# Changeover between two feed-forward layers: one weight conversion later, a load asked for earlier, output tiles kept apart

## The chip, the cores and the metric

One core of a Trainium2 chip runs the whole program. The metric is the device time in microseconds (us) of one execution; three runs of the kernel before took 1017.71, 1018.67 and 1021.01 us, and the median is 1018.67 us. All the arithmetic is in fp32, and the matrix products are built from fp32r halves ("hi" and "lo" of a number), three matmuls for one product.

## The reference

Causal attention with a bias from a cumulative sum (4 batches, 8 heads, 576 positions, head dimension 64), then two feed-forward layers on 2304 tokens, 512 wide, 2048 hidden:

```python
x = attention(q, k, v, s)              # -> (2304, 512)
h = x @ w_in1;  g = max(h, 0) + alpha * min(h, 0);   y = g @ w_out1
h = y @ w_in2;  g = h * clip(h + 3, 0, 6) / 6;       out = g @ w_out2
```

The weights arrive as float64 and are turned into fp32 on the chip.

## The kernel before, in words

Attention and layer one are interleaved (lines 744 to 818). Layer one runs over blocks of 256 tokens; its last pass, which the change touches, takes the last two blocks at once, 512 tokens (`moe1`, line 660, called at line 850). For each of 16 slices f of the hidden width it makes 12 matmuls into a bank `h` (line 248), then ScalarE and VectorE turn `h` into `gt` (lines 697 and 698), ScalarE rounds it to `gh` (line 701), VectorE makes the rest `gl` (line 702), and 12 matmuls add `gh` and `gl` into the four banks `y` (line 675). The y products of a slice follow the h products of the next one (skew 1). After slice 15 the four banks are copied to `yt` tiles (line 684, pool `stg`, two buffers) and stored to the scratch tensor `y_scratch` (line 686). `f` below counts these slices: gt14 is `gt` of slice 14.

During this last pass the weights of layer two's first product are loaded and converted, in eight pairs, called p0 to p7 here (`load_pair`, line 192; `split_pair`, line 213, called from `more_w2`, line 723). The raw words `wraw` are float64. A conversion of a pair is, per half: ScalarE line 142 writes `wcv`, GpSimd lines 144 and 147, VectorE line 152, and then the low bits, by VectorE at line 155 or by ScalarE at line 150 (`by`, chosen by the last argument of `to_f32`). GpSimd then forms sums `ws` (lines 180 to 183), and ScalarE and VectorE split everything into hi and lo `wc` (lines 160 and 161). `ws` has one buffer, which the token sums `yt` of layer two share (tag "ws").

Layer two's first product uses a scheme of seven products instead of eight (`Step`, line 856). Tokens go in four groups g of 576, hidden columns in eight places j, one pair of weights each; `order` (line 954) begins with group 0, j = 0 to 2, then group 1, all j. A step is 42 matmuls of 128x288 (line 872) in the banks a, b and c, ended by ScalarE copies to `z` and `m5` (`held`, line 879), VectorE additions (`plus`, line 882), and the gate (lines 885 and 886) into `gt2` tiles that are stored to `g_scratch` (line 891). In the trace m5 appears as m and gt2 as gt. The tokens of a group are read back from `y_scratch` (`load_x`, line 826; DMA line 832 into `yr`, two buffers), summed by GpSimd (lines 187 to 190) and split (lines 160 and 161) into x. Groups 0 and 1 use different x tiles; the one of group 1 lies where tiles of layer one's last pass were.

The last phase (lines 1007 to 1039) multiplies the stored g by the second weights w_out2, 16 slices f per block of 512 tokens. These weights are loaded by `load_out` into tiles of first-layer weights that are free (`places`, line 934) and converted by `split_out`.

Memory is given out by pools as stacks from the left and the right side. `stg` is the first pool of the stack `layer1`, which is closed at line 854; pool `m2` of layer two (z, three buffers, and gt2, four) is opened on the left right after that, and so lies where `stg` was. Instructions are put in order on each engine when the program is built; the order follows the text with priorities (`tc.high_priority`), and a converted pair that stands in layer two's loop (line 971) can be placed earlier than the loop's first matmul. All these DMAs are issued by the SP queue, one after the other; an issue that waits holds those behind it.

## Time and profile before

| what | value |
|---|---|
| median of three runs | 1018.67 us (1017.71 to 1021.01) |
| the profiled execution, its own time | 1021.8 us |
| its span, first to last instruction | 1020.0 us |
| TensorE matmuls busy | 984.2 us (96%), 6218 matmuls |
| VectorE, ScalarE, GpSimd busy | 619.9, 630.0, 443.4 us |
| mean granted clock of TensorE | 0.977 of full speed |
| chain of waits, share of TensorE | 90% |

The busy times are of one profiled execution, which took 3.1 us more than the median of the three runs. TensorE is busy nearly all the time, so the time of the kernel is the sum of TensorE's work and of the stretches in which TensorE waits or runs at its lower clock. The layers change over between 611 and 650 us of the span.

### The profile page before, as it was taken

Reading aid. Unit: us, or ns where it says so; the run is one execution under the profiler, and the core shown is the slowest. Engines: PE = TensorE matmul, PEld = TensorE weight load, DVE = VectorE, ACT = ScalarE, POOL = GpSimd, SP = SyncE. Lnnn points to the kernel's source line nnn. Section 1 sums busy time; section 2 is a strip of 40 time slices with the busy share of each in tenths; the row PEclk is TensorE's granted clock in tenths of the full one; section 3 lists DMA queues with packets and bytes.
Section 4 is the critical chain, followed back from the end, with each engine's and each line's share of the span. In section 5 each row is a group of like instructions: output and inputs, shape, how many; then the busy total and the mean of one; then the engine's idle time right before and its main releaser. Section 6 shows DMA issues by size and latency. Waiting matters only on the chain.

```text
span 1020.0 us, 18068 instructions
## 1 busy us (share of the span) xinstructions
PE 984.2 (96%) x6218; PEld 883.1 (87%) x6218; DVE 619.9 (61%) x1507; ACT 630.0 (62%) x1429; POOL 443.4 (43%) x587
## 2 busy tenths in 40 slices
PE   8889999999999999999999996999999999999998
PEld 5568788999999989998998884999999988888886
DVE  5678884556766666666656895757667872222222
ACT  6568778678778788777755544656657653232322
POOL 5554667657667666657636765402203220000000
PEclk9779999999999999999999998899999999999999
DMA  6890014112212122222106321334337733332412
GB/s 209 290 356 4 24 30 130 40 46 89 75 62 84 53 80 68 64 83 75 33 8 215 96 94 58 142 124 150 118 146 279 273 129 124 115 133 83 161 59 90
DMA packets 59829, 114.47 MB, mean 112 GB/s; under 512 B 5705, under 2 KB 21881, under 8 KB 59737
## 3 DMA queue, kind: packets, MB, share of 16 engines
q1 hardware_dynamic: 59736, 113.32, 33.6%
q8 instruction: 49, 0.80, 0.3%
q14 instruction: 44, 0.35, 0.1%
HBM read 84.84 MB, written 28.46 MB: 111 GB/s over the span
## 4 chain that ended last, share of the span: by engine, by line
PE 90%; DVE 2%; ACT 2%; issue 2%; DMA 1%; POOL 1%; SPq 0%; ACTq 0%; POOLq 0%; DVEq 0%
PE o L1029 19%; PE h L248 19%; PE y L675 19%; PE a L872 10%; PE b L872 5%; PE s L410 4%; PE pv L472 4%; PE pt L447 4%; PE c L872 3%; PE s L322 1%; PE pv L603 1%; DMA wraw<-in_w_in 1%; PE pt L593 1%; PE h L534 1%; DVE wcv L152 1%
## 5 line engine op out<-in xcount | busy, mean ns | idle before, releaser
L248 PE MATMUL h<-xhi,wi 128*128 128x256 f32 (+1 forms) x896 | 227.7, 322 | 2.8 <-DVE gt L698 1.6
L1029 PE MATMUL o<-wo,gh 128*128 128x512 f32 x576 | 173.7, 389 | 1.1 <-DVE gt L886 1.1
L248 PEld LDWEIGHTS h<-xhi,wi 128*128 128x128 f32 x896 | 156.9, 192 | 16.2 <-DVE gt L698 1.9
L675 PE MATMUL y<-gh,wo 128*128 128x256 f32 (+1 forms) x896 | 164.0, 318 | 4.8 <-ACT gh L701 4.8
L675 PEld LDWEIGHTS y<-gh,wo 128*128 128x128 f32 x896 | 134.6, 191 | 17.2 <-ACT gh L701 6.3
L248 PE MATMUL h<-xlo,wi 128*128 128x256 f32 (+1 forms) x448 | 143.6, 321 | 0.0
L161 DVE TENSOR_TENSOR gl<-gr,gh 128x512 fp32r<-128x512 f32 (+1 forms) x80 | 51.3, 643 | 130.1 <-ACT gh L160 113.8
L1029 PEld LDWEIGHTS o<-wo,gh 128*128 128x128 f32 x576 | 107.9, 188 | 23.5 <-DVE gt L886 1.3
L144 POOL TENSOR_SCALAR wcv<-wcv 128x512 f32<-128x512 f32 x64 | 48.4, 763 | 170.6 <-ACT wcv L142 167.7
L160 ACT ACTIVATE gh<-gr 128x512 fp32r<-128x512 f32 (+1 forms) x80 | 47.0, 590 | 121.8 <-PE o L1029 121.8
L872 PE MATMUL a<-x,wc 128*128 128x288 f32 x768 | 115.4, 299 | 6.2 <-ACT z L879 6.2
L872 PEld LDWEIGHTS a<-x,wc 128*128 128x128 f32 x768 | 108.4, 192 | 6.9 <-ACT z L879 6.4
L1029 PE MATMUL o<-wo,gl 128*128 128x512 f32 x288 | 108.1, 389 | 0.0
L675 PE MATMUL y<-gl,wo 128*128 128x256 f32 (+1 forms) x448 | 92.4, 319 | 0.0
L248 PEld LDWEIGHTS h<-xlo,wi 128*128 128x128 f32 x448 | 86.0, 192 | 5.9
L422 POOL TENSOR_SCALAR t<-t,rec 128x384 f32<-128x384 f32 (+2 forms) x96 | 65.7, 686 | 57.2 <-DVE rec L421 32.8
L413 DVE CUSTOM_DVE_ANT_0 t<-s,mask 128x384 f32<-128x384 f32 (+2 forms) x96 | 53.4, 563 | 54.6 <-PE pt L447 35.5
L698 DVE SCALAR_TENSOR_TENSOR gt<-gt,beta,h 128x256 f32<-128x256 f32 (+1 forms) x112 | 61.6, 552 | 30.2 <-ACT gt L697 29.1
L418 ACT ACTIVATE t<-t,m 128x384 f32<-128x384 f32 (+2 forms) x96 | 67.2, 701 | 17.0 <-DVE m L413 15.8
L675 PEld LDWEIGHTS y<-gl,wo 128*128 128x128 f32 x448 | 70.3, 191 | 6.2 <-issue 0.2
L702 POOL TENSOR_TENSOR gl<-gt,gh 128x256 fp32r<-128x256 f32 x80 | 59.3, 742 | 30.5 <-ACT gh L701 28.6
L383 POOL TENSOR_TENSOR ks<-kraw,ks 64x576 fp32r<-64x576 f32 (+1 forms) x40 | 52.6, 1316 | 41.1 <-issue 33.5
(135 smaller groups left out, 2015.3 us busy)
## 6 DMA issues: line engine op xcount, KB each, us to landing
g_scratch<-gt SPq DMA_DIRECT2D x64, 288.0 KB
wraw<-in_w_in SPq DMA_DIRECT2D x32, 512.0 KB
wraw<-in_w_out SPq DMA_DIRECT2D x32, 512.0 KB
gr<-g_scratch SPq DMA_DIRECT2D x16, 1024.0 KB
kraw<-in_kt SPq DMA_DIRECT2D x32, 288.0 KB
qraw<-in_qt SPq DMA_DIRECT2D x32, 160.0 KB
vraw<-in_vp SPq DMA_DIRECT2D x32, 160.0 KB
y_scratch<-yt SPq DMA_DIRECT2D x18, 256.0 KB
```

The costliest lines, as they stand in the source:

```text
L144: keep(nc.gpsimd.tensor_scalar(cf, cf, W_MOST, -W_MOST, op0=ALU.min, op1=ALU.max))
L161: keep(nc.vector.tensor_tensor(lo, of, hi.bitcast(F32), op=ALU.subtract))
L248: nc.tensor.matmul(dst, lt, r, start=first and i == 0, stop=last and i == len(terms) - 1)
L383: nc.gpsimd.tensor_tensor(ks[D:P], kraw[D:P], ks[D:P].bitcast(F32), op=ALU.subtract)
L413: nc.vector.tensor_tensor_reduce(t[:n, a:e], sc[:n, : e - a], mask[:n, MASK + n - (e - a) :][:, : e - a] if e == w else mask[:n, : e - a], ...
L418: nc.scalar.activation(t[:n, :w], t[:n, :w], AF.Exp, bias=m[-1][:n], scale=-1.0, accum_out=den[:n])
L422: nc.gpsimd.tensor_scalar(t[:n, :w], t[:n, :w], rec[:n], 1.0, op0=ALU.mult, op1=ALU.mult)
L675: nc.tensor.matmul(ys[dc // per][:, o : o + n], which[:, dc * P : (dc + 1) * P], gg, start=(f == 0 and which is wl and dc % per == 0), sto ...
L698: nc.vector.scalar_tensor_tensor(gt, gt, beta[:, f : f + 1], hp[:, :n], op0=ALU.mult, op1=ALU.add)
L702: (nc.vector if n == 512 else nc.gpsimd).tensor_tensor(gl, gt, gh.bitcast(F32), op=ALU.subtract)
L872: nc.tensor.matmul(dst[:, :NX2], lt, r, start=first and n == 0, stop=n == len(terms) - 1, skip_group_check=not first,)
L1029: nc.tensor.matmul(op[i], lt[:, tsl], r, start=(f == 0 and r is wh and lt is gh), stop=(f == FC - 1 and lt is gl))
```

## The change

Layer one's output pool `stg` moves from the stack `layer1` (left side) to the right side and lives until the end; the output tiles `ot` of the last phase now use its two buffers instead of a pool of their own. In the last pass five weight pairs are converted instead of six, and the sixth, p5, moves into layer two's loop ahead of the seventh and eighth (at i = 1, 3, 5 instead of two pairs at 1 and 3). For pairs that are converted in the last pass the low bits of the first half are now made by ScalarE (line 150) instead of VectorE (line 155). The loads of the second token group are written out in layer one's loop (`load_raw(1)` at f = 8). The third buffer of `z` and the fourth of `gt2` now lie in two free weight tiles, wo11 and wo31 (`turn_of`), which were the first two places of the w_out2 weights; those two go to the end of the list, so that fourteen of the sixteen are loaded during layer two's first product and the last two as the last phase begins. Line numbers grow by up to 13 (872 becomes 879, 879 becomes 886, 832 becomes 833).

```diff
@@ -86,8 +86,8 @@
     edge = ctx.enter_context(tc.tile_pool(name="edge", bufs=1, side="right"))
     wp = ctx.enter_context(tc.tile_pool(name="wp", bufs=1))
     ps = ctx.enter_context(tc.tile_pool(name="ps", bufs=1, space=PSUM))
+    stg = ctx.enter_context(tc.tile_pool(name="stg", bufs=2, side="right"))
     layer1 = ctx.enter_context(ExitStack())
-    stg = layer1.enter_context(tc.tile_pool(name="stg", bufs=2))
     ring = layer1.enter_context(tc.tile_pool(name="ring", bufs=1))
 
 
@@ -213,7 +213,7 @@
     def split_pair(pair, pool, bufs, pin=False):
         keep = tc.keep_in_program_order if pin else (lambda ins: ins)
         j, raw = pair
-        c0, c1 = to_f32(raw, pool, "wcv", bufs, keep, (False, False))
+        c0, c1 = to_f32(raw, pool, "wcv", bufs, keep, (bufs == WB, False))
         q = [c.rearrange("p (k h f) -> p h k f", k=2, h=2) for c in (c0, c1)]
         s = pre.tile([P, 3, 2, P], F32, tag="ws", bufs=1, name="ws")
         s_forms(nc.gpsimd, q[0][:, 0], q[0][:, 1], q[1][:, 0], q[1][:, 1], [s[:, i] for i in range(3)], keep)
@@ -724,7 +724,7 @@
 
         if f >= 2 and f % 2 == 0 and len(units2) < NU:
             units2.append(load_pair(w_in2, len(units2)))
-        if f >= 6 and f % 2 == 0 and len(w2) < NU:
+        if f >= 6 and f % 2 == 0 and len(w2) < 5:
             with tc.high_priority(offset=W2P):
                 w2.append(split_pair(units2[len(w2)], pool, pool.wb))
 
@@ -823,16 +823,21 @@
     NJ = FC // 2
     FORMS = ((0, 0), (2, 2), (6, 3), (3, 6), (4, 4), (5, 5), (1, 1))
 
+    raws = {}
+
+    def load_raw(g):
+
+        rows = y_d[:, g * 2 * NX2 : (g + 1) * 2 * NX2].rearrange("(s k p) t -> k p s t", s=2, k=2)
+        raws[g] = [pre.tile([P, 4, NX2], F32, tag="yr", bufs=2, name="yr") for k in range(2)]
+        for k, yr in enumerate(raws[g]):
+            nc.sync.dma_start(yr.rearrange("p (s h) t -> p s (h t)", s=2), rows[k])
+
     def load_x(pool, g):
 
-        raws = []
-        rows = y_d[:, g * 2 * NX2 : (g + 1) * 2 * NX2].rearrange("(s k p) t -> k p s t", s=2, k=2)
-        for k in range(2):
-            yr = pre.tile([P, 4, NX2], F32, tag="yr", bufs=2, name="yr")
-            nc.sync.dma_start(yr.rearrange("p (s h) t -> p s (h t)", s=2), rows[k])
-            raws.append(yr)
+        if g not in raws:
+            load_raw(g)
         x = pool.tile([P, 2, 2, 7, NX2], F32R, tag="x", bufs=1, name="x2")
-        for k, yr in enumerate(raws):
+        for k, yr in enumerate(raws[g]):
             yt = pre.tile([P, 3, NX2], F32, tag="ws", bufs=1, name="yt2")
             t_forms(nc.gpsimd, *[yr[:, i] for i in range(4)], [yt[:, i] for i in range(3)])
             split(x[:, 0, k, :4], x[:, 1, k, :4], yr)
@@ -850,6 +855,8 @@
         for f, _ in enumerate(moe1(w1, (NBLK - 2, NBLK - 1), pool, ("g5", "gh5", "gl5", 2), 1)):
             if f == 4:
                 xs[0] = load_x(xa, 0)
+            if f == 8:
+                load_raw(1)
             more_w2(f, pool)
     layer1.close()
 
@@ -892,7 +899,7 @@
 
         def first(self):
             self.a = bank("a")
-            self.z = m2.tile([P, 2 * NX2], F32, tag="z", bufs=3, name="z")
+            self.z = turn_of("z", 2, "wo11")
             self.product(1, self.a, True)
             self.held(self.z[:, :NX2], self.a)
 
@@ -914,13 +921,13 @@
         def seventh(self):
             self.product(7, self.a, False)
             self.plus(self.m5, self.a)
-            self.gt = m2.tile([P, 2 * NX2], F32, tag="gt", bufs=4, name="gt2")
+            self.gt = turn_of("gt", 3, "wo31")
             self.gate(self.gt[:, NX2:], self.m5)
 
         def third(self):
             self.product(3, self.b, False)
             self.plus(self.z[:, NX2:], self.b)
-            gt = m2.tile([P, 2 * NX2], F32, tag="gt", bufs=4, name="gt2")
+            gt = turn_of("gt", 3, "wo31")
             self.gate(gt, self.z)
             self.store(0, gt)
 
@@ -929,13 +936,23 @@
             self.gate(self.gt[:, :NX2], self.a[:, :NX2])
             self.store(1, self.gt)
 
+    turns = {}
+
+    def turn_of(tag, n, place):
+
+        turns[tag] = turns.get(tag, -1) + 1
+        if turns[tag] % (n + 1) == n:
+            return wp.tile([P, 2 * NX2], F32, tag=place, name=tag)
+        return m2.tile([P, 2 * NX2], F32, tag=tag, bufs=n, name=tag)
+
     wo2, outs = [], []
 
-    places = [("wo11", 0), ("wo31", 0)]
+    places = []
     for j in range(4):
         places += [(f"{nm}{j}{i}", j) for nm, i in (("wi", 0), ("wi", 1), ("wo", 0))]
         if j % 2:
             places.append((f"wo{j - 1}1", j))
+    places += [("wo31", 3), ("wo11", 3)]
 
     def load_out(f):
 
@@ -968,7 +985,7 @@
         xs[1] = load_x(xb, 1)
         last = None
         for i, (g, j) in enumerate(order):
-            if i in (1, 3):
+            if i in (1, 3, 5):
                 with tc.high_priority(offset=WLP):
                     w2.append(split_pair(units2[len(w2)], cv, 2))
             if i == ends[1] + 2:
@@ -978,14 +995,9 @@
             if i == ends[2] + 2:
                 xbs.close()
                 gp = late.enter_context(tc.tile_pool(name="late", bufs=2))
-            if i in (8, 10):
-                load_out(len(outs))
-            if i in (14, 18):
-                with tc.high_priority(offset=WLP):
-                    split_out(len(wo2))
             if i >= ends["w", 0] + 2:
                 for _ in range(2):
-                    if len(outs) < FC and i >= ends["w", places[len(outs)][1]] + 2:
+                    if len(outs) < FC - 2 and i >= ends["w", places[len(outs)][1]] + 2:
                         load_out(len(outs))
                 if len(wo2) < len(outs) - 1:
                     with tc.high_priority(offset=WLP):
@@ -1003,7 +1015,6 @@
         last.third()
         last.fourth()
         right.close()
-        m3 = late.enter_context(tc.tile_pool(name="out2", bufs=2, side="right"))
         stage(o=[0, 1, 2, 3, 4, 5, 6, 7])
         NB2 = 512
         GC = 4
@@ -1012,6 +1023,8 @@
             ntt = n // P
             op = [bank("o") for i in range(ntt)]
             for f in range(FC):
+                if bi == 0 and f < 2:
+                    load_out(len(outs))
                 if bi == 0 and len(wo2) < FC and f % 2 == 0:
                     split_out(len(wo2))
                 if f % GC == 0:
@@ -1030,7 +1043,7 @@
                             op[i], lt[:, tsl], r, start=(f == 0 and r is wh and lt is gh), stop=(f == FC - 1 and lt is gl)
                         )
             for i in range(ntt):
-                ot = m3.tile([P, DM], F32, tag="ot", name="ot")
+                ot = stg.tile([P, DM], F32, tag="yt", name="ot")
                 nc.scalar.activation(ot, op[i], AF.Copy, scale=1.0 / 6.0)
                 at = 0
                 for t, m in rows_of(t0 + i * P, P):
```

The change moves instructions at three places.

First, VectorE at the end of layer one's last pass (gt and gl are those of slices 14 and 15, lines 152 and 155 the conversion of a pair). Before:

```order
L702 TENSOR_TENSOR gl<-gt,gh 128x512
L152 SCALAR_TENSOR_TENSOR wcv<-wcv,wraw 128x512
L155 SCALAR_TENSOR_TENSOR wcv<-wraw,wcv 128x512
L152 SCALAR_TENSOR_TENSOR wcv<-wcv,wraw 128x512
L155 SCALAR_TENSOR_TENSOR wcv<-wraw,wcv 128x512
L698 SCALAR_TENSOR_TENSOR gt<-gt,beta,h 128x512
L161 TENSOR_TENSOR wc<-wcv,wc 128x512
L702 TENSOR_TENSOR gl<-gt,gh 128x512
L161 TENSOR_TENSOR x_8708<-yr,x_8708 128x1152
```

and with the change, on the same engine from gl13 on:

```order
L702 TENSOR_TENSOR gl<-gt,gh 128x512
L152 SCALAR_TENSOR_TENSOR wcv<-wcv,wraw 128x512 x2
L155 SCALAR_TENSOR_TENSOR wcv<-wraw,wcv 128x512
L698 SCALAR_TENSOR_TENSOR gt<-gt,beta,h 128x512
L155 SCALAR_TENSOR_TENSOR wcv<-wraw,wcv 128x512
L702 TENSOR_TENSOR gl<-gt,gh 128x512
L161 TENSOR_TENSOR wc<-wcv,wc 128x512
L698 SCALAR_TENSOR_TENSOR gt<-gt,beta,h 128x512
L702 TENSOR_TENSOR gl<-gt,gh 128x512
L161 TENSOR_TENSOR x_8679<-yr,x_8679 128x1152
```

Before, four conversion instructions (of p6, the seventh pair) stand in one row between gl14 and gt15; with the change four (of p5) stand around gt14, three ahead of it and one behind, and one hi/lo split ahead of gt15.

Second, ScalarE at the changeover, from the first copies of the y banks on. Before:

```order
L684 ACTIVATE yt<-y 128x512 x2
L160 ACTIVATE x_8708<-yr 128x1152
L160 ACTIVATE x_8708<-yt_8709 128x864
L684 ACTIVATE yt<-y 128x512
L879 ACTIVATE m_8697<-b 128x288
L684 ACTIVATE yt<-y 128x512
L160 ACTIVATE x_8708<-yr 128x1152
L879 ACTIVATE z<-a 128x288
L160 ACTIVATE x_8708<-yt_8718 128x864
L879 ACTIVATE z<-a 128x288 x2
```

and with the change:

```order
L684 ACTIVATE yt<-y 128x512 x2
L160 ACTIVATE x_8679<-yr 128x1152
L160 ACTIVATE x_8679<-yt_8680 128x864
L886 ACTIVATE z<-a 128x288
L684 ACTIVATE yt<-y 128x512
L886 ACTIVATE m_8672<-b 128x288
L684 ACTIVATE yt<-y 128x512
L886 ACTIVATE z<-a 128x288 x2
L892 ACTIVATE gt<-m_8672,three 128x288
L160 ACTIVATE x_8679<-yr 128x1152
```

The first copy to z moves ahead of the third and fourth copy of y and of the second half of x.

Third, the SP queue from layer one's last token loads to the end of the changeover (yr are the loads of token groups 0, 1 and 2, wraw the raw weights). Before:

```order
L197 DMA wraw<-in_w_in 128x1024
L832 DMA yr<-y_scratch 128x2x576 x2
L197 DMA wraw<-in_w_in 128x1024 x4
L832 DMA yr<-y_scratch 128x2x576
L197 DMA wraw<-in_w_in 128x1024
L832 DMA yr<-y_scratch 128x2x576
L197 DMA wraw<-in_w_in 128x1024 x8
L686 DMA y_scratch<-yt 128x512 x3
L832 DMA yr<-y_scratch 128x2x576
L686 DMA y_scratch<-yt 128x512
L197 DMA wraw<-in_w_in 128x1024 x2
```

and with the change:

```order
L197 DMA wraw<-in_w_in 128x1024
L833 DMA yr<-y_scratch 128x2x576 x2
L197 DMA wraw<-in_w_in 128x1024 x4
L833 DMA yr<-y_scratch 128x2x576
L197 DMA wraw<-in_w_in 128x1024
L833 DMA yr<-y_scratch 128x2x576
L197 DMA wraw<-in_w_in 128x1024 x8
L686 DMA y_scratch<-yt 128x512 x2
L833 DMA yr<-y_scratch 128x2x576
L686 DMA y_scratch<-yt 128x512 x2
L197 DMA wraw<-in_w_in 128x1024 x2
```

The two loads of token group 1 (the third and fourth yr) keep their place; the first load of group 2 moves ahead of the third store of y.

## Rows read from the trace of the kernel before

**Rows 1.** Windows: stretch, length, busy us per engine (instructions), granted clock, DMA share, GB/s.

```profile
620.00:630.00 10.00, 6.07 (x17) 4.51 (x16) 5.38 (x7) 2.11 (x4) 4.16 (x4) 0.70 0.00 0
640.00:650.00 10.00, 10.00 (x62) 10.00 (x61) 6.13 (x11) 6.24 (x14) 5.94 (x8) 0.77 0.25 82
```

**Rows 2.** Waits of TensorE, 540 to 1020 us: total us, times, longest.

```profile
PE a L872 <- ACT z L879: 6.2, 1, 6.2
PE y L675 <- ACT gh L701: 4.8, 2, 3.9
...
PE o L1029 <- DVE gt L886: 1.1, 1, 1.1
```

**Rows 3.** Timeline of TensorE, changeover: start, us, operation, count [idle before <- releaser].

```profile
616.66 0.39 PE L248 MATMUL h<-xhi,wi 128*128 128x512 f32 x1
617.93 2.12 PE L675 MATMUL y<-gh,wo 128*128 128x512 f32 x8 [0.88 <-ACT gh L701]
...
624.88 3.78 PE L675 MATMUL y<-gh,wo 128*128 128x512 f32 x8 [3.93 <-ACT gh L701]
...
639.25 4.69 PE L872 MATMUL a<-x,wc 128*128 128x288 f32 x18 [6.18 <-ACT z L879]
...
644.92 0.96 PE L872 MATMUL b<-x,wc 128*128 128x288 f32 x6
645.71 0.96 PE L872 MATMUL a<-x,wc 128*128 128x288 f32 x6
```

**Rows 4.** Timeline, end of layer one: ScalarE, GpSimd and VectorE.

```profile
617.78 0.58 ACT L697 ACTIVATE gt<-h 128x512 f32<-128x512 f32 x1
...
618.30 1.23 POOL L187 TENSOR_TENSOR yt<-yr 128x288 f32<-128x288 f32 x1
618.78 1.29 DVE L152 SCALAR_TENSOR_TENSOR wcv<-wcv,wraw 128x512 uint32<-128x512 uint32 x1
...
623.42 0.73 DVE L698 SCALAR_TENSOR_TENSOR gt<-gt,beta,h 128x512 f32<-128x512 f32 x1
...
624.19 0.63 ACT L701 ACTIVATE gh<-gt 128x512 fp32r<-128x512 f32 x1
```

**Rows 5.** Timeline, changeover: ScalarE and the SP queue.

```profile
629.12 1.08 ACT L684 ACTIVATE yt<-y 128x512 f32<-128x512 f32 x2 [4.29 <-PE y L675]
...
632.33 0.58 ACT L684 ACTIVATE yt<-y 128x512 f32<-128x512 f32 x1
...
634.02 0.32 SPq L686 DMA_DIRECT2D y_scratch<-yt  x1
...
638.78 0.41 ACT L879 ACTIVATE z<-a 128x288 f32<-128x288 f32 x1 [1.12 <-DMA y_scratch<-yt]
```

**Rows 6.** Groups by form, 545 to 660 us (busy, mean ns), and line 150 (min/median/max).

```profile
L152 DVE SCALAR_TENSOR_TENSOR wcv<-wcv,wraw 128x512 uint32<-128x512 uint32 x16 | 16.7, 1053 | 1.4 <-POOL wraw L147 1.4
L155 DVE SCALAR_TENSOR_TENSOR wcv<-wraw,wcv 128x512 uint32<-128x512 uint32 x16 | 14.8, 930 | 0.1
...
L147 POOL TENSOR_SCALAR wraw<-wcv 128x512 f32<-128x512 f32 x16 | 15.0, 949 | 0.7
L144 POOL TENSOR_SCALAR wcv<-wcv 128x512 f32<-128x512 f32 x15 | 12.6, 844 | 10.1 <-ACT wcv L142 7.7 <-issue 2.2
...
L150 ACT ACTIVATE wraw<-wraw x12: 1358/1374/1389, 78.2 to 140.6; 128x512 uint16<-128x512 uint16 x12
```

**Rows 7.** Timelines of ScalarE and TensorE around slice 12's gh and y products.

```profile
604.02 0.63 ACT L701 ACTIVATE gh<-gt 128x512 fp32r<-128x512 f32 x1 [0.82 <-DVE gt L698]
...
607.11 1.98 PE L675 MATMUL y<-gh,wo 128*128 128x512 f32 x8
608.92 1.07 PE L675 MATMUL y<-gl,wo 128*128 128x512 f32 x4
```

**Rows 8.** Timeline of the SP queue: the two loads of token group 1.

```profile
551.56 0.38 SPq L832 DMA_DIRECT2D yr<-y_scratch  x1
...
565.32 0.38 SPq L832 DMA_DIRECT2D yr<-y_scratch  x1
```

## The prediction, as put on record before the changed kernel ran

> **What bounds the kernel now.** I read the windows view first. TensorE is busy in almost every stretch; the exception is the changeover between the layers, where it is busy 6.07 of 10 us at a granted clock of 0.70, and 20 us later still runs at 0.77 of full speed, that is, part of the time at the lower of its two levels, 1.2 instead of 2.4 GHz [rows 1]. The view of TensorE's waits names what it waited for: 4.8 us for gh of layer one and 6.2 us for z of layer two; from there to the end of the kernel only 1.1 us more [rows 2]. So the change is worth what it does to these two waits and to the slow clock behind them.
>
> The timeline of TensorE gives the size. The last h matmul starts at 616.66, and the second b product of layer two at 644.92 [rows 3]. A wide matmul follows the next at 0.226 us (eight in 1.81 [rows 7]), so the h work ends at 616.89 and the stretch is 28.0 us long. It holds 24 wide matmuls (y14 and y15), 5.4 us, and 42 narrow ones, which at 0.132 us (six in 0.79 [rows 3]) are 5.5 us. That makes 11.0 us of work and **17.0 us lost**: waits of 0.88, 3.93 and 6.18 [rows 3], together 11.0, and 6.0 us because TensorE came back slow. After the wait of 3.93 eight wide matmuls took 3.78 us, not 1.98 [rows 3, 7], and after that of 6.18 eighteen narrow ones took 4.69, or 0.26 each [rows 3].
>
> **Why the two waits are there.** ScalarE had gt15 ready from 617.78 + 0.58, but VectorE came to its part only at 623.42, because four instructions of p6's conversion stood before it from 618.78 on, the later ones waiting for GpSimd, which had a token sum of 1.23 us between its own two conversion steps [rows 4]. gh15 followed at 624.19 and y15 at 624.88 [rows 3, 4]. The second wait: ScalarE could not write z because m2 lies over the yt tiles of layer one; the last store of yt was issued at 634.02 and let z go at 638.78, that is 4.76 us later [rows 5].
>
> **The change, part by part.** *Output tiles on the right side.* z now lies where the ring of layer one's inputs was, last read by the h matmul of 616.66 [rows 3]. The wait for the store goes. Next is late what stands ahead of z on ScalarE: two copies of y and both first pieces of x, which took 629.12 to 632.33 [rows 5], 3.21 us, and z itself 0.41, so z is there 3.62 us after the first copy starts. TensorE in that time has three more wide matmuls (0.68) and eighteen narrow ones (2.38), 3.06 in all. New wait: 0.6. The seventh product of the first step then needs z of the sixth, which stands behind two more y copies (0.58 each [rows 5]), one of m and its own (0.41 each), 1.98 us, against 1.58 of TensorE (twelve narrow): 0.4. If the third y copy must first see the first store land, and that takes the 4.76 us of the last one, 1.8 more. In rows 5 the third copy started directly behind the x pieces, with no idle time noted, so I stay near the lower end: **1.5 us of new waits**, bounds 1.0 and 2.8, and zero if TensorE itself is later.
>
> *p5 instead of p6 at the tail.* The order shows that the move does not empty the tail: p5 is pulled forward into it as p6 was, but stands one slice earlier and is spread over two slices. I walk it from the end of h12. gt12 is done after 0.58 + 0.73 [rows 4] = 1.3; two splits behind it at some 0.93 each, 3.2. Then ws is free, and GpSimd does four token sums (1.23 each [rows 4]), two of line 144 and two of line 147 (0.844 and 0.949 [rows 6]): 11.7. Behind these VectorE's second line 152, 1.05, and line 155, 0.93 [rows 6], gt14, 0.73, and gh14, 0.63 [rows 4]: 15.0. TensorE, counted in its new order, has 72 wide matmuls from h12 to y14, 16.3 us: 1.3 to spare. From gt14 (14.4) another line 155, gl14 and a split at 0.93 each, gt15 and gh15: 18.6, against y15 at 16.3 + 2.7 = 19.0: 0.4 to spare. So both waits for gh go, thinly.
>
> *Low bits on ScalarE.* Five instructions of 1.37 us in place of five of 0.93 on VectorE [rows 6]. ScalarE now stands still until GpSimd has done two of line 144 and one of line 147, 2.64 us; with line 150 that is 4.0 us per pair. Behind it in the queue is a gh; in rows 7 gh12 was ready at 604.65 and needed at 607.11, 2.46 us to spare. I take zero, since VectorE, relieved of 4.65 us, delivers gt earlier, and in the new order three of the five stand right behind a gh; upper end 5 x (4.0 - 2.46) = 7.8 us.
>
> *The second tokens.* Both loads were issued at 551.56 and 565.32 already [rows 8], and stand at the same place of the SP queue with the change: zero. The first load of group 2 moves ahead of two y stores; those now hold nothing that TensorE needs.
>
> *The rest.* z and gt2 keep three and four buffers, zero. Three pairs instead of two are finished in layer two: p5 is due in step 8, eight steps of 42 x 0.132 = 5.5 us away, so TensorE's own work covers it; without cover it costs about the GpSimd chain above, 8.5 us. Two loads of 512 KB and two conversions move to the start of the last phase. The weights of f = 14 are due 14 x 12 x 0.226 = 38 us after it begins; a store of half that size took 4.76 us [rows 5], so even 9.5 is covered. The output tiles have two buffers as before.
>
> **Sum.** 17.0 - 1.5 = 15.5 us. Against the profiled execution's own time, 1021.8 (span 1020.0, 1.8 around it): 1006.3. The median of the three runs is 3.1 lower, 1018.67, and the loss is inside the span of every execution, so the median should come to **1003.2**. With new waits between 0 and 2.8 and about 1 us of spread, 1001 to 1005.5.
>
> **The rivals.** *The tail still waits.* What is to spare for y14 and y15 is 1.3 and 0.4 us. Line 152 took 1.29 beside a token sum of GpSimd [rows 4] and 1.053 in the mean [rows 6]; if every VectorE step of the chain must outwait a GpSimd instruction, the four ahead of gh14 take some 1.23 more each, 4.9, and TensorE waits 3.6 us, about the old 3.93. With twelve wide matmuls at 0.45 behind it (2.7) that is 6.6 us kept: 1009.8. Chance 0.14. The Trainium skill ("SBUF — State Buffer", section "SBUF: two separate sides") calls the port that VectorE and GpSimd share a lock held for a whole instruction, which would make it come out like this; the trace agrees as far as the 1.29 goes.
>
> *z still waits at the changeover*, because something else under the new place is released late. 6.18 is kept, and 2.3 of slow clock (4.69 - 2.38), in place of my 1.5: 1010.2. The ring's last reader at 616.66 speaks against it. Chance 0.04.
>
> *Line 150 holds gh in every pair* (the other side). With 4.0 against 2.46 to spare it costs 7.8: 1011.0, chance 0.04. It decides against the change when each of the five costs 3.1 us (15.5 / 5), that is, when the chain on ScalarE grows from 4.0 to 5.6; around there, 1016 to 1021, chance 0.03. If each wait reaches 3.93, TensorE comes back slow as in rows 3, and five times 3.93 + 2.7 = 33 us are lost: 1036, chance 0.03. For it: gh14 was 0.88 late as it was [rows 3]. Against it: ScalarE is busy in only 2.11 and 6.24 of 10 us in the windows of rows 1.
>
> *The change doesn't do what it says*: true of the tokens, which cost nothing either way, and partly of p5; it is the first rival.
>
> **How the numbers follow.** My forecast has 0.72, the rivals 0.14, 0.04 and 0.10. Runs of this kernel tell 0.3%, about 3 us, from no change. Faster by more than that is all below 1015.6: 0.72 + 0.14 + 0.04 + 0.04 = 0.94; same 0.03; slower 0.03. The range takes in the forecast and the first two rivals: 1000.5 to 1010.5.
>
> **What would show it.** In the profile after: no wait of y for gh over 1 us; z written directly behind the x pieces, with no DMA as its releaser; windows of TensorE at 10 of 10 us and clock 1.00 through the changeover; from the last h to the second b product some 12.5 us. A wait of TensorE on gh in the last pass with line 150 ahead of it on ScalarE, or y14 behind line 152, would make it wrong.

## The result, and the profile after

The changed kernel takes **1003.4 us** (median of 4 runs, 1001.04 to 1003.67), the kernel before 1018.93 us beside it (4 runs, 1017.71 to 1021.01): a ratio of 0.984, with a 95% interval of 0.9818 to 0.9862. The prediction was 1003.2 us, 1000.5 to 1010.5, and faster with a chance of 0.94. It held.

The windows of the changeover in the profile after (stretch, length, busy us of PE, PEld, DVE, ACT, POOL with their instructions, granted clock, DMA share, GB/s), which answer to [rows 1]:

```profile
610.00:620.00 10.00, 10.00 (x53) 8.64 (x52) 5.06 (x8) 5.12 (x8) 0.00 (x0) 1.00 0.12 44
620.00:630.00 10.00, 9.73 (x74) 9.50 (x73) 8.17 (x13) 7.64 (x16) 4.88 (x6) 1.00 0.78 258
```

Before, [rows 1] show 6.07 of 10 us at 0.70; the emptiest window, which they leave out, is the next one, and it holds the whole wait of 6.18 us for z:

```profile
630.00:640.00 10.00, 3.82 (x22) 3.48 (x22) 4.14 (x4) 5.95 (x9) 3.08 (x4) 0.84 0.76 253
```

The worst window is now 9.73 of 10 us at full clock, and those from 630 to 650 us are at 10.00 and 1.00. The waits of TensorE from 540 us to the end of the same execution (total us, times, longest), to be held against [rows 2]:

```profile
PE o L1042 <- DVE gt L893: 1.1, 1, 1.1
PE a L879 <- ACT z L886: 0.3, 1, 0.3
```

Of 4.8 and 6.2 us of waits, 0.3 is left at the changeover; the 1.1 at the gate of the last phase, which the change doesn't touch, stands as it did. The timeline of TensorE in the changed kernel (start, us, operation, count, [idle before <- releaser]), for [rows 3]:

```profile
612.20 0.39 PE L248 MATMUL h<-xhi,wi 128*128 128x512 f32 x1
612.42 1.98 PE L675 MATMUL y<-gh,wo 128*128 128x512 f32 x8
...
615.14 1.98 PE L675 MATMUL y<-gh,wo 128*128 128x512 f32 x8
...
619.46 0.96 PE L879 MATMUL b<-x,wc 128*128 128x288 f32 x6
620.68 2.66 PE L879 MATMUL a<-x,wc 128*128 128x288 f32 x18 [0.27 <-ACT z L886]
...
623.97 0.96 PE L879 MATMUL b<-x,wc 128*128 128x288 f32 x6
```

Eight wide matmuls take 1.98 us and eighteen narrow ones 2.66, where 3.78 and 4.69 stood [rows 3]. The last h matmul ends at 612.20 + 0.226 = 612.43 and the second b product starts at 623.97: the stretch is **11.54 us** long, against 28.0 before.

**Where the time went.** I cut each profiled execution in three: up to the end of the last h matmul, the stretch, and from the second b product to the end of the span (us; worked out from each trace as in the prediction; labels are those of the experiments below).

| kernel | up to last h | stretch | behind it | span | median of the runs |
|---|---|---|---|---|---|
| before | 616.9 | 28.0 | 375.1 | 1020.0 | 1018.93 |
| changed | 612.4 | 11.54 | 375.3 | 999.3 | 1003.4 |
| changed, a second time | 614.6 | 11.54 | 375.3 | 1001.4 | 1003.18 |
| tiles alone (e1) | 613.7 | 19.25 | 375.3 | 1008.2 | 1011.1 |
| change, tiles undone (e2) | 616.9 | 20.56 | 375.2 | 1012.7 | 1010.6 |
| change, low bits undone (e3) | 616.4 | 11.87 | 376.3 | 1004.5 | 1005.19 |
| change, tokens undone (e4) | 616.9 | 11.55 | 375.9 | 1004.4 | 1004.22 |
| change, pair undone (e5) | 613.5 | 19.6 | 376.5 | 1009.6 | 1009.82 |
| before, with filler (e6) | 614.1 | 25.5 | 376.4 | 1016.1 | 1018.32 |
| before, buffers alone (e7) | 615.2 | 27.9 | 375.1 | 1018.2 | 1019.22 |
| change, order of banks (e8) | 613.3 | 11.54 | 374.1 | 998.9 | 1000.97 |
| the same, a second time (e10) | 616.8 | 11.62 | 374.0 | 1002.4 | 1003.44 |

Two things are to be seen. What the change gives, 16.5 us, lies in the stretch; the 375 us behind it differ by 0.2. (Where the part behind is 0.6 to 1.3 us longer, in e3 to e6, TensorE waits 0.45 to 1.16 us more for a z late in layer two; see e6.) And the part ahead of it scatters from 612.4 to 616.9 us, also between two executions of one kernel (612.4 and 614.6; 613.3 and 616.8), so a whole time tells 3 us poorly, while the stretch repeats to 0.1 us. In the experiments the stretch is the measure and the median its check. One run of the kernel before, taken beside e9 and e10, lasted 1597.67 us at a mean granted clock of 0.555, where the other eight there show 0.978 to 0.984, and nothing below is worked out from it.

### The profile page after: what moved, and what is told of

The parts are those of the page before. It is cut to its first block, busy times and chain, and to the rows that moved or that the text cites. A ratio compares the mean times of both kernels' runs of the same rounds, so it can differ in the third digit from the quotient of the medians.

```text
span 999.3 us, 18072 instructions
## 1 busy us (share of the span) xinstructions
PE 972.0 (97%) x6218; PEld 873.5 (87%) x6218; DVE 614.2 (61%) x1502; ACT 633.0 (63%) x1434; POOL 439.4 (44%) x587
## 4 chain that ended last, share of the span: by engine, by line
PE 93%; DMA 2%; ACT 2%; issue 1%; DVE 1%; SPq 0%; POOL 0%; ACTq 0%; DVEq 0%; POOLq 0%
PE y L675 20%; PE h L248 20%; PE o L1042 20%; PE a L879 10%; PE b L879 5%; PE s L410 4%; PE pv L472 4%; PE pt L447 4%; PE c L879 2%; PE s L322 2%; DMA vraw<-in_vs 1%; DMA kr<-cum_scratch 1%; PE h L534 1%; PE pv L603 1%; DMA wraw<-in_w_out 1%
## 5 line engine op out<-in xcount | busy, mean ns | idle before, releaser
L248 PEld LDWEIGHTS h<-xhi,wi 128*128 128x128 f32 x896 | 156.4, 191 | 16.4 <-DVE gt L698 1.9
L675 PE MATMUL y<-gh,wo 128*128 128x256 f32 (+1 forms) x896 | 162.0, 315 | 0.0
L879 PE MATMUL a<-x,wc 128*128 128x288 f32 x768 | 112.9, 295 | 0.3 <-ACT z L886 0.3
L879 PEld LDWEIGHTS a<-x,wc 128*128 128x128 f32 x768 | 106.0, 188 | 0.8 <-ACT z L886 0.5
L418 ACT ACTIVATE t<-t,m 128x384 f32<-128x384 f32 (+2 forms) x96 | 67.1, 700 | 17.0 <-DVE m L413 15.8
L701 ACT ACTIVATE gh<-gt 128x256 fp32r<-128x256 f32 (+1 forms) x112 | 53.1, 476 | 29.3 <-DVE gt L698 27.7
```

The lines of the kernel that those rows point to most:

```text
L248: nc.tensor.matmul(dst, lt, r, start=first and i == 0, stop=last and i == len(terms) - 1)
L418: nc.scalar.activation(t[:n, :w], t[:n, :w], AF.Exp, bias=m[-1][:n], scale=-1.0, accum_out=den[:n])
L675: nc.tensor.matmul(ys[dc // per][:, o : o + n], which[:, dc * P : (dc + 1) * P], gg, start=(f == 0 and which is wl and dc % per == 0), sto ...
L701: nc.scalar.activation(gh, gt, AF.Copy)
L879: nc.tensor.matmul(dst[:, :NX2], lt, r, start=first and n == 0, stop=n == len(terms) - 1, skip_group_check=not first,)
```

## The experiments

Theory A is the prediction's: the two waits are separate losses; each costs its own length and the slow matmuls behind it, and each goes with its own part of the change (the wait for z with the tiles, the waits for gh with p5's place).

**e1, the tiles alone.** The borrowed buffers, which make room for the tiles, stay; pair, low bits and tokens go back:

```diff
-        c0, c1 = to_f32(raw, pool, "wcv", bufs, keep, (bufs == WB, False))
+        c0, c1 = to_f32(raw, pool, "wcv", bufs, keep, (False, False))
...
-        if f >= 6 and f % 2 == 0 and len(w2) < 5:
+        if f >= 6 and f % 2 == 0 and len(w2) < NU:
...
-            if f == 8:
-                load_raw(1)
...
-            if i in (1, 3, 5):
+            if i in (1, 3):
```

> The kernel with the change, with the other three edits undone: six pairs in layer one's last pass, low bits on VectorE, the second tokens as before. Only the output tiles' memory (and the two borrowed buffers that make room for it) is left of the change. Theory A, separate losses: each wait costs its own length and the slow clock behind it. The wait for z (6.2 us, plus about 2.9 us of narrow matmuls at 0.26 instead of 0.13) goes, the wait for gh15 (3.9) with its slow clock stays: from the last h to the second b product 19 us instead of 28.0 and 11.5; time about 1010. Theory B, one slow stretch: TensorE is still slow from the first wait when it reaches layer two, so that the narrow matmuls stay at 0.26 and only the wait itself is earned: about 22 us for the stretch, time about 1013.

Measured: 1011.1 us (5 runs) against 1018.51 of before, ratio 0.9918, 95% 0.9891 to 0.9945. Timeline of TensorE in this kernel:

```profile
614.71 2.11 PE L675 MATMUL y<-gh,wo 128*128 128x512 f32 x8 [0.87 <-ACT gh L701]
...
621.67 3.78 PE L675 MATMUL y<-gh,wo 128*128 128x512 f32 x8 [3.94 <-ACT gh L701]
...
629.75 2.55 PE L877 MATMUL a<-x,wc 128*128 128x288 f32 x18
```

The waits for gh stand as in [rows 3], to 0.01 us; the wait for z is gone altogether, and the eighteen narrow matmuls run at full clock. The stretch is 8.8 us shorter. So the tiles take away the second wait and nothing else.

**e2, the change with its tiles undone.** `stg` goes back into `layer1`, and the output tiles into a pool of their own:

```diff
-    stg = ctx.enter_context(tc.tile_pool(name="stg", bufs=2, side="right"))
     layer1 = ctx.enter_context(ExitStack())
+    stg = layer1.enter_context(tc.tile_pool(name="stg", bufs=2))
```

> The kernel with the change, only the output tiles put back where they were. Theory A: the wait for z is back with some 6 to 7 us, and the narrow matmuls behind it are slow (2.9 us), while the end of layer one stays without a wait: from the last h to the second b product about 20 us, time about 1012. Theory B: without the first wait TensorE comes to the second at full clock, keeps it through part of the wait, and loses only the wait: about 18 us, time about 1010; if the clock needs both waits to fall, the narrow matmuls stay at 0.13.

Measured: 1010.6 us (5 runs), ratio 0.9923, 95% 0.9892 to 0.9954. Timeline of this kernel, TensorE, the SP queue and ScalarE:

```profile
619.68 1.98 PE L675 MATMUL y<-gh,wo 128*128 128x512 f32 x8
...
624.00 0.96 PE L879 MATMUL b<-x,wc 128*128 128x288 f32 x6
...
626.28 0.46 SPq L686 DMA_DIRECT2D y_scratch<-yt  x1
...
631.09 0.41 ACT L886 ACTIVATE z<-a 128x288 f32<-128x288 f32 x1 [0.98 <-DMA y_scratch<-yt]
...
631.55 4.69 PE L879 MATMUL a<-x,wc 128*128 128x288 f32 x18 [6.59 <-ACT z L886]
```

The mirror image: no wait for gh, and z waits for the last store of y as in [rows 5], here 631.09 - 626.28 = 4.81 us behind its issue (4.76 before). TensorE came to this wait at full clock and left it slow: 4.69 us for eighteen. The stretch is 7.5 us shorter than before. 8.8 and 7.5 make 16.3, and both together gave 16.5: the two losses add up, as theory A says. The medians say 7.4 and 7.9, together 15.3, against 15.5.

**e3, the low bits undone.** VectorE makes all low bits again; the rest of the change stays:

```diff
-        c0, c1 = to_f32(raw, pool, "wcv", bufs, keep, (bufs == WB, False))
+        c0, c1 = to_f32(raw, pool, "wcv", bufs, keep, (False, False))
```

> The kernel with the change, only the low bits of the first half back on VectorE (five instructions of 0.93 us there instead of five of 1.37 on ScalarE). Theory A: the move of the pair alone frees the tail; y14 or y15 waits at most 0.5 us, no slow clock, time 1003 to 1004.5. Theory B: it is ScalarE's line 150 that keeps VectorE on time; without it gt14 or gt15 is late again by 2 to 4 us, TensorE comes back slow, time 1007 to 1010.

Measured: 1005.19 us (4 runs, 1003.05 to 1006.24), ratio 0.9853, 95% 0.982 to 0.9886. Timeline of ScalarE and TensorE in this kernel:

```profile
615.83 0.63 ACT L701 ACTIVATE gh<-gt 128x512 fp32r<-128x512 f32 x1 [4.07 <-DVE gt L698]
...
616.12 0.39 PE L248 MATMUL h<-xhi,wi 128*128 128x512 f32 x1
...
616.52 2.11 PE L675 MATMUL y<-gh,wo 128*128 128x512 f32 x8
```

y14 now starts 0.17 us late (616.52 against 616.35, where h ends), as gh14 ends at 616.46, and the stretch is 0.33 longer. Line 150 on ScalarE therefore gives a little, a third of a microsecond; whether the whole time shows it can't be told from these runs.

**e4, the tokens undone.** The two lines `if f == 8: load_raw(1)` are taken out.

> The kernel with the change, only the early load of the second tokens taken out. Theory A: both loads were issued 60 us before they are used already in the kernel before, so nothing moves: time within 1 us of the kernel with the change, and the same stretch of 11.5 us. Theory B: the early request is part of what made x of group 1 ready in time; without it step 3 of layer two waits 2 us or more, time 1005.5 or more.

Measured: 1004.22 us (4 runs, 1001.59 to 1007.19), ratio 0.9841, 95% 0.9796 to 0.9886. The stretch is 11.55 us, that of the change to 0.01: asking in layer one's text for what was already asked for there gives nothing.

**e5, the pair undone.** Six pairs in the last pass again, low bits on ScalarE and the tiles as changed:

```diff
-        if f >= 6 and f % 2 == 0 and len(w2) < 5:
+        if f >= 6 and f % 2 == 0 and len(w2) < NU:
...
-            if i in (1, 3, 5):
+            if i in (1, 3):
```

> The kernel with the change, only the sixth pair back in layer one's last pass, so that the seventh stands at its tail between gl14 and gt15 as before; the low bits stay on ScalarE, the tiles stay apart. Theory A: the place of the pair makes the tail's wait; y15 waits about 3 to 4 us for gh15 and runs at the lower clock behind it, from the last h to the second b product 18 to 19.5 us, time about 1010. Theory B: the relief of VectorE by line 150 suffices; y15 waits under 1 us, the stretch stays under 13 us, time 1003 to 1005.

Measured: 1009.82 us (4 runs) against 1018.03, ratio 0.9903, 95% 0.987 to 0.9935. Timeline of TensorE in this kernel:

```profile
615.77 2.14 PE L675 MATMUL y<-gh,wo 128*128 128x512 f32 x8 [2.10 <-ACT gh L701]
...
621.92 3.78 PE L675 MATMUL y<-gh,wo 128*128 128x512 f32 x8 [3.09 <-ACT gh L701]
```

The waits for gh are back, 5.2 us in all, as 2.10 and 3.09 instead of 0.87 and 3.94. The stretch is 19.6 us against 19.25 of e1, where the low bits were undone as well. So it is the move of the pair that takes away the waits of the tail; without it the low bits on ScalarE only move some of the wait from y15 to y14.

**e6, a filler in the wait for z.** To test the second half of theory A, that the slow matmuls follow from the idle time, the kernel before gets 40 matmuls into a free bank that nothing reads (work added, nothing left out):

```diff
+                    for n in range(40):
+                        tc.keep_in_program_order(
+                            nc.tensor.matmul(spare[:, :NX2], w2[0][0][0][:, 0], x0[:, 0, 0, 0], start=True, stop=True, skip_group_check=True)
+                        )
+                    step.sixth()
```

> The kernel before, with 40 narrow matmuls of no use (their bank is never read) put on TensorE behind the first three products of layer two, where it waits 6.2 us for z; 40 times 0.132 is 5.3 us, so they fit into the wait. The wait for z itself stays: z is written at the same time. Theory A: TensorE comes out of the wait at its full clock, since it was busy in it; the 18 and 6 narrow matmuls behind it take 0.13 each instead of 0.26 and 0.2, and the kernel is 2.5 to 3 us faster than before although it does more work: about 1016. Theory C: the slow matmuls behind the wait come from something else than idleness (operands, banks, the other engines' traffic); they stay at 0.26, time as before, 1018.5, or later by what the 40 matmuls overrun.

Measured: 1018.32 us (10 runs) against 1018.03, ratio 0.9988, 95% 0.9971 to 1.0004: by the whole time no change that could be told, and not the 1016 I had expected. Timeline of TensorE in this kernel:

```profile
629.86 5.43 PE L1001 MATMUL spare<-x,wc 128*128 128x288 f32 x40
636.39 2.66 PE L872 MATMUL a<-x,wc 128*128 128x288 f32 x18 [1.10 <-ACT z L879]
...
803.61 1.06 PE L872 MATMUL a<-x,wc 128*128 128x288 f32 x6 [1.16 <-ACT z L879]
```

The stretch does what theory A says. z comes no earlier, but the eighteen matmuls behind it take 2.66 us instead of 4.69, and the stretch is 2.5 us shorter (25.5). The part behind the stretch is 1.3 us longer than before, most of it by the wait of 1.16 us for another z, 170 us later. ScalarE ahead of that z, with the filler and, in the second row, in the kernel before:

```profile
801.20 1.67 ACT L160 ACTIVATE gh<-gr 128x512 fp32r<-128x512 f32 x3 [2.22 <-DMA gr<-g_scratch]
...
804.11 1.66 ACT L160 ACTIVATE gh<-gr 128x512 fp32r<-128x512 f32 x3
```

With the filler ScalarE stood still for a load of g; in the kernel before it did not. That the filler is the cause isn't shown: at the same product e3, e4 and e5, which have no filler, wait 0.68, 0.45 and 0.96 us behind the same load, and between two executions of one kernel (e8 and e10) ScalarE's wait for it is none and 0.35 us. The interval of the ratio goes from 3.0 us faster to 0.4 slower, so the whole time neither shows nor rules out the 2.5 us of the stretch. The slow clock behind this wait is thus shown to come from the idle time; what the filler gives at the end of the kernel is left open.

**e7, the borrowed buffers alone.** The kernel before with `turn_of`, `places` and the two late loads, and nothing else of the change that has an effect (the lines that loaded and converted the first w_out2 weights at i = 8, 10, 14 and 18 are gone, as in the change):

```diff
-            self.z = m2.tile([P, 2 * NX2], F32, tag="z", bufs=3, name="z")
+            self.z = turn_of("z", 2, "wo11")
...
-    places = [("wo11", 0), ("wo31", 0)]
+    places = []
...
+    places += [("wo31", 3), ("wo11", 3)]
...
+                if bi == 0 and f < 2:
+                    load_out(len(outs))
```

> The kernel before, with only the borrowed buffers of the change: the third z and the fourth gt2 in the tiles wo11 and wo31, fourteen of the weights of the last phase loaded later in layer two's first product and two as the last phase begins. Theory A: free of cost, time 1018.5 within 1.5 us, the waits of 0.9, 3.9 and 6.2 us as before, none new in the last phase. Theory B: the two late loads and conversions hold the last phase; a new wait of TensorE of 1 us or more there, time 1020 or more.

Measured: 1019.22 us (10 runs), ratio 1.0017, 95% 1.0 to 1.0033; stretch 27.9, behind it 375.1, and no wait that before doesn't have. They cost at most the 0.3% that a measurement can tell, and nothing that the trace shows.

**e8, a version that could be better.** In the changed kernel one wait is left late, 1.1 us of bank o for the gate: the first bank that the last phase opens is one that the gate is still reading. Another order of the banks:

```diff
-        stage(o=[0, 1, 2, 3, 4, 5, 6, 7])
+        stage(o=[2, 5, 7, 0, 3, 6, 4, 1])
```

> The kernel with the change, with the last phase's banks taken in another order (2, 5, 7, 0, 3, 6, 4, 1 instead of 0 to 7), so that its first products don't go into the bank that the last gate of layer two still reads. Theory A: the one wait left there, 1.1 us for that gate, goes; time 1 us under the kernel with the change, about 1002.4, less than the runs can tell from it. Rival: the wait moves to the next thing late there, the second slice's gl or the first token load of the phase; time as with the change, 1003.4.

Measured: 1000.97 us (4 runs, 1000.48 to 1001.33) against 1018.03, ratio 0.9828, 95% 0.9806 to 0.985. The only wait of TensorE from 540 us on is the 0.3 for z. But the gap to the change's 1003.4 is no larger than the scatter of the first part, so both were run again, side by side on one chip.

**e9 and e10, the change and that version side by side.** No edit beyond those above.

> The changed kernel without any edit, timed once more beside the order of banks on the same chip. Theory A: 1003.4 as before, within 2, and the stretch from the last h to the second b product again 11.5 us with the wait for z of layer two under 0.5. Rival: the 11.5 us were one lucky execution; then the spare of 0.54 and 0.42 us that gh14 and gh15 had is gone in this profile and a wait of y for gh shows, 1 us or more.

> The changed kernel with the banks of the last phase staged in the order 2, 5, 7, 0, 3, 6, 4, 1, once more, beside the changed kernel. Theory A: the one wait of 1.1 us of the last phase's first bank for the gate goes, so 1.1 us faster than the changed kernel by the same call's medians, 0.5 to 2.5. Rival: the 1000.97 measured before is the scatter of the first part of the kernel; then the two medians lie within 0.5 us of one another or in the other order.

Measured: the change 1003.18 us (5 runs, 1002.2 to 1003.9), ratio 0.9839 with 95% 0.982 to 0.9858; the order of banks 1003.44 us (5 runs, 1000.94 to 1005.63), ratio 0.984 with 95% 0.9814 to 0.9866; the kernel before, beside both, 1019.6 (8 runs). The timeline of TensorE in the repeated change:

```profile
614.36 0.39 PE L248 MATMUL h<-xhi,wi 128*128 128x512 f32 x1
614.59 1.98 PE L675 MATMUL y<-gh,wo 128*128 128x512 f32 x8
...
622.85 2.65 PE L879 MATMUL a<-x,wc 128*128 128x288 f32 x18 [0.27 <-ACT z L886]
...
626.13 0.96 PE L879 MATMUL b<-x,wc 128*128 128x288 f32 x6
```

The stretch repeats, 11.54 us with the same 0.27 for z, so the result of the change is no lucky execution. In the trace of the version with the banks the wait of 1.1 us is gone again, 374.0 us behind the stretch against 375.3. The medians lie 0.26 us apart, in the other order: theory A's 0.5 to 2.5 us did not come, and the rival's sign, medians within 0.5 us, did. Whether that version is faster by the whole time is left open.

## Why the prediction was right

**The mechanism** held in each step: the stretch was the whole of the gain (16.5 us of it, nothing behind), both waits went, each with its own part of the change (e1, e2, e5), and the slow clock went with them (e6). The rest cost nothing that shows: tokens (e4), borrowed buffers and late loads (e7). z stands directly behind the x pieces, with no DMA as its releaser, and no window of the changeover is below full clock.

**The term that was mis-sized** is the "1.5 us of new waits"; 0.27 of it came as a wait, and 0.5 in all (11.54 us of stretch less the prediction's 11.0 of work), so that the stretch is 11.54 us in place of some 12.5. ScalarE and the SP queue at the changeover, in the changed kernel:

```profile
617.38 1.09 ACT L684 ACTIVATE yt<-y 128x512 f32<-128x512 f32 x2 [2.66 <-PE y L675]
618.01 0.81 SPq L686 DMA_DIRECT2D y_scratch<-yt  x2
618.35 1.17 ACT L160 ACTIVATE x<-yr 128x1152 fp32r<-128x1152 f32 x1
619.40 0.93 ACT L160 ACTIVATE x<-yt 128x864 fp32r<-128x864 f32 x1
620.23 0.40 ACT L886 ACTIVATE z<-a 128x288 f32<-128x288 f32 x1
620.51 0.61 ACT L684 ACTIVATE yt<-y 128x512 f32<-128x512 f32 x1
...
621.28 0.63 ACT L684 ACTIVATE yt<-y 128x512 f32<-128x512 f32 x1
621.79 0.42 ACT L886 ACTIVATE z<-a 128x288 f32<-128x288 f32 x1
```

I had added whole durations, but instructions in a row overlap: the next one starts before the end of the one ahead. From the first y copy to the end of z it is 620.63 - 617.38 = 3.25 us, not 3.62; that is most of what made the 0.6 a 0.27. From the third y copy to the end of the second z it is 622.21 - 620.51 = 1.70, not 1.98, and TensorE shows no wait there: the 0.4 made zero. And the upper bound, a third y copy that waits 4.76 us for the first store, did not come: it started 2.50 us after that store was issued, without idle time ahead of it.

**The walk through the tail** came out right by luck, with two errors against one another. Tail of the changed kernel, ScalarE, VectorE and GpSimd:

```profile
598.53 0.63 ACT L160 ACTIVATE wc<-ws 128x512 fp32r<-128x512 f32 x1 [2.32 <-POOL ws L181]
599.07 0.58 ACT L697 ACTIVATE gt<-h 128x512 f32<-128x512 f32 x1
600.37 0.74 DVE L698 SCALAR_TENSOR_TENSOR gt<-gt,beta,h 128x512 f32<-128x512 f32 x1
...
602.12 1.19 POOL L187 TENSOR_TENSOR yt<-yr 128x288 f32<-128x288 f32 x1 [2.23 <-DVE wc L161]
603.39 0.81 POOL L188 TENSOR_TENSOR yt<-yr,yt 128x288 f32<-128x288 f32 x1
603.41 0.75 DVE L698 SCALAR_TENSOR_TENSOR gt<-gt,beta,h 128x512 f32<-128x512 f32 x1 [0.77 <-ACT gt L697]
...
607.57 1.26 POOL L147 TENSOR_SCALAR wraw<-wcv 128x512 f32<-128x512 f32 x2
608.25 1.71 DVE L152 SCALAR_TENSOR_TENSOR wcv<-wcv,wraw 128x512 uint32<-128x512 uint32 x2 [2.70 <-POOL wraw L147]
609.88 0.68 DVE L155 SCALAR_TENSOR_TENSOR wcv<-wraw,wcv 128x512 uint32<-128x512 uint32 x1
610.48 0.74 DVE L698 SCALAR_TENSOR_TENSOR gt<-gt,beta,h 128x512 f32<-128x512 f32 x1
611.25 0.63 ACT L701 ACTIVATE gh<-gt 128x512 fp32r<-128x512 f32 x1 [3.41 <-DVE gt L698]
...
614.09 0.63 ACT L701 ACTIVATE gh<-gt 128x512 fp32r<-128x512 f32 x1 [0.81 <-DVE gt L698]
```

By the prediction's own count h12 ended 16.3 us before y14, at 612.42 - 16.3 = 596.1. gt12 was then done at 601.11, 5.0 us later and not 1.3, because on ScalarE a hi/lo split stood ahead of it and waited 2.32 us for GpSimd, and on VectorE another, of 1.25 us, followed. So GpSimd began 6.0 us after h12 (602.12 - 596.1), not 3.2. But it needed 6.7 us for its eight instructions (602.12 to 608.83), not 8.5. gh14 came 15.8 us after h12, not 15.0: **0.54 us to spare instead of 1.3**. For gh15 it is 615.14 - 614.72 = 0.42, and 0.4 was forecast. The spare is thin indeed: in e9 gh14 had 0.30, and without the low bits (e3) y14 started 0.17 late.

**The rivals.** *The tail still waits* had the right mechanism and the wrong place. (Its 6.6 us kept are a slip: the 3.6 and 2.7 it adds make 6.3.) In the kernel before, the rows look as if VectorE and GpSimd outwait one another; these rows, of its timeline, go on where [rows 4] stop:

```profile
619.49 1.09 POOL L147 TENSOR_SCALAR wraw<-wcv 128x512 f32<-128x512 f32 x1
620.11 1.00 DVE L155 SCALAR_TENSOR_TENSOR wcv<-wraw,wcv 128x512 uint32<-128x512 uint32 x1
620.55 1.21 POOL L188 TENSOR_TENSOR yt<-yr,yt 128x288 f32<-128x288 f32 x1
621.03 1.27 DVE L152 SCALAR_TENSOR_TENSOR wcv<-wcv,wraw 128x512 uint32<-128x512 uint32 x1
```

Each starts while the other engine is at work, and ends 0.53 to 0.65 us after the other has ended (620.58, 621.11, 621.76, 622.30). In the changed kernel line 155 takes 0.68 at 609.88, with GpSimd idle. A token sum takes 0.81 at 603.39 though VectorE is at work beside it, but on line 698, whose large inputs are one tile (gt) and the bank h; line 155 reads two tiles. The Trainium skill ("SBUF — State Buffer", section "SBUF: two separate sides") calls the port that both engines use an exclusive lock for a whole instruction, and counts only such instructions of VectorE as have two inputs in SBUF, or run in a mode with two ports, among those that take it; these rows agree with it, as a reading of overlaps, though no run here took the lock away. This lengthening did not decide against the change since there GpSimd has finished its sums and conversions, at 608.83, when VectorE comes to most of its part, and the window of 610 to 620 us shows GpSimd at 0.00.

*z still waits* came only where I undid the tiles (e2). *Line 150 holds gh*: there are 17 of them now, five more, at a median of 1.37 us, and no wait for gh in the last pass; they give 0.33 us in the stretch. *The change doesn't do what it says*: true of the tokens, as forecast. Its words put p5 into the second layer; most of p5's conversion still stands in the tail, and what helped, as the rows read, is that it stands one slice earlier. A p5 wholly behind the last pass wasn't tried.

**The time** came nearer than its parts: 15.5 us forecast in the stretch, 16.5 measured there, 15.5 by the first medians and 16.4 by those of e9 (1019.6 - 1003.18). The last three agree within the scatter of the first part; that a forecast 1 us off in the stretch came within 0.2 us of the median is luck.

## What to carry to other kernels

Where the engine that sets the time is busy elsewhere, measure a change by the stretch in which it idles, from one fixed instruction to another; whole times of several hundred us carry a scatter that has nothing to do with the change. Price such a stall as its length and, where the clock falls, the slow matmuls behind it, and free a buffer's successor from a store by giving it other memory. Before adding up durations on a queue, look at start times: rows that follow one another overlap.

## What the runs showed of the hardware

The clock after a wait was not in proportion to the wait. Behind waits of 0.87 and 2.10 us eight wide matmuls took 2.11 and 2.14 us (e1, e5); behind 3.09, 3.93 and 3.94 they took 3.78 each time (e5, before, e1). Behind 6.18 and 6.59, eighteen narrow ones took 4.69 both times (before, e2), though TensorE had come to the second at full clock. In e5 the window from 620 to 630 us shows a granted clock of 0.66 for it, in the changed kernel 1.00. With 40 useless matmuls and a wait of 1.10 instead of 6.18, they took 2.66 (e6). Nor does the wait alone decide. Two executions of the changed kernel (the first, then e9) show the same waits of 0.78 and 0.33 us at some 459 us, and behind them the same four matmuls:

```profile
461.61 0.69 PE L472 MATMUL pv<-ptl,vs 128*128 128x320 f32 x4
...
462.83 1.16 PE L472 MATMUL pv<-ptl,vs 128*128 128x320 f32 x4
```

The granted clock from 460 to 465 us is 1.00 in the first and 0.70 in the second.

I had not expected one instruction to have so many prices: in the changed kernel line 155 took 0.67 to 1.22 us, a token sum 0.81 to 1.29, in the rows above by what the other engine was at work on. In a group's mean (930 ns for line 155 in [rows 6]) both kinds are mixed, and a walk built on the mean is right only by luck.

Not expected either was the scatter of the part ahead of the stretch, 612.4 to 616.9 us for kernels whose order there is the same or nearly so. The traces show two places of it. At one wait of TensorE for gt, near the beginning, the twelve executions already stand between 171.90 (before with filler) and 175.78 us (e3), the kernel before at 175.17, though the filler comes 450 us later. And the two executions of the change are 0.86 us apart there (172.30 and 173.16) and 2.16 at the last h; the other 1.3 us come about from 460 to 466 us, where the clock fell in one of them only. Why it fell there, and what moves the first 170 us, stays open.
